# Chunked attention and a SoLU feed-forward: two single rows instead of four, two more units transposed on TensorE, one run per partition for q, k, v, few fillers, a new order of steps

## The chip, the cores and the metric

The kernel runs on one core of one Trainium2 chip. The metric is device time in microseconds of one execution. Before the change three runs gave 383.9, 387.94 and 388.43 us, median 387.94. Names of engines: PE is TensorE (PEld its weight loads), DVE VectorE, ACT ScalarE, POOL GpSimd; SP is the engine that issues nearly all DMAs.

## The reference

Attention over chunks, then a feed-forward layer, on 4 x 768 = 3072 tokens of width 512 (8 heads of 64):

```python
for c in range(nc):                       # 32 queries at a time
    k_ctx = k[:, :, l_start:r_end]        # 16 keys to the left, 8 to the right of the chunk
    k_full = np.concatenate([mem_k, k_ctx], axis=2)          # and 8 memory keys
    v_full = np.concatenate([mem_v, v_ctx], axis=2)
    scores = scale * np.matmul(q_c, k_full.transpose(0, 1, 3, 2))
    a = softmax(scores)
    out[:, :, c_start:c_end] = np.matmul(a, v_full)
...
h = x @ w_in                              # x: 3072 x 512, w_in: 512 x 1024
sm = softmax(h)
solu = h * sm
ln = (solu - mean) / np.sqrt(var + 1e-06) * g_ln
return ln @ w_out                         # w_out: 1024 x 512
```

The two weight matrices arrive as 64-bit floats, 4 MB each; everything else is 32-bit.

## The kernel before, in words

The 3072 tokens are 24 rows of tiles of 128 tokens. In the attention part an item is one row (items 0 to 3) or two rows (items 4 to 13). In the feed-forward part the unit is always one row, t = 0 to 23. The whole program is straight-line code: a string `ORDER` (line 29) lists about a thousand steps by short names, and the loop at line 569 issues them in just that order. So the order of instructions on each engine's queue is the order of the string, and each engine works through its own queue strictly in turn, waiting on semaphores where a step needs data or a free buffer.

Attention, for item i: `Lq`, `Lk`, `Lv` load q, k and v (SP, line 226). `S` computes the scores, 32 small fp32 matmuls per row (line 347; each shows as two matmul and two weight-load instructions). `M`, `Bm`, `X`, `Z` are the row maximum, its subtraction, the exponential (ScalarE) and the reciprocal row sum. The probabilities are then transposed: either on TensorE (`PT`, line 333, and a copy `PC` out of PSUM), or, for paired items, by VectorE in 32 x 32 blocks (`Pt`, line 304), a write to DRAM (`Pw`, line 312) and four reads of 128 KB that put the blocks in place (`Pr`, line 320). `V` multiplies by v (line 415), `N` normalises. The result x is transposed in the same two ways (`XT`, or `Xt`, `Xw`, `Xr`), and `XH`, `XL` round it to a high part and a residual.

Feed-forward, for row t: `Gt.c.half` are the hidden matmuls, a group of three per step (high x high, high x low, low x high; line 480), 8 groups per row. `Hm`, `He`, `Hu` are maximum, exponential and product; `C` centres; the row is transposed on TensorE (`UT`, rows 0 to 3) or through DRAM (`Ut`, `Uw`, `Ur`); `UH`, `UL` split it; `Ot.f` are the projection matmuls, 8 groups of three (line 540); `Sq`, `Dn` make the variance and its root, `Os` scales the result (line 548) and `St` stores it, from ScalarE's queue.

Weights: `D` loads a piece (SP), `A` packs its upper words (ScalarE, line 261), `B` shifts (line 268) and `I` inserts the lower words (VectorE, line 273), `H` and `L` split it into a rounded part and a residual (lines 214, 217, 282). The pieces are two halves of w_in's first chunk of 128 rows, its three other chunks, and four pairs of w_out's blocks.

`Wu n` are fillers: n multiplications of a zero tile by itself (line 201), each of which shows as two matmul instructions. A letter behind @ names the engine of a step that can run on several: V VectorE, S ScalarE, G POOL.

Of the kernel before, what the change touches and what calls it, by code (L numbers as in the profile page):

```python
# [11 lines left out]
F32 = mybir.dt.float32  # L12
# [6 lines left out]
P = 128  # L19
# [4 lines left out]
SINGLES = 4  # L24
# [5 lines left out]
CT Lk0 Wu18 Lq0 S0 M0 Bm0 Wu19 D0 A0 B0 I0 H0.0@G L0.0@G X0 Z0 PT0 PC0@S D1 A1 Lq2 Lk2 S2 M2 Bm2 X2  # L30
B1 I1 H1.0@G Z2 Lk1 Lq1 S1 M1 D4 A4 B4 I4 Wu36 Lv0 D2 A2 Lk3 V0 Wu28 Bm1 L1.0@G N0 B2 Lq3 I2 H2.1@G
XT0 XH0@S Lv2 S3 PT2 PC2@S H4.0@G M3 XL0@V V2 Bm3 G0.0.0 X1 PT1 Z1 G0.0.1 X3 PT3 H2.0@G N2 PC1@S
PC3@S Lv1 Z3 D3 V1 A3 N1 L2.0@G G0.1.0 B3 I3 L4.0@G Lv3 V3 N3 XT2 XH2@S XL2@V XT1 L2.1@G Lk4 Lq4
G0.1.1 S4 M4 XH1@S XL1@V H3.0@G G2.0.0 G2.0.1 G2.1.0 H3.1@S D6 A6 XT3 XH3@S Bm4 D7 H4.1@G L3.0@G
L3.1@G G0.2.0 G0.2.1 B6 XL3@V G1.0.0 I6 X4 Pt4 D5 A5 B5 I5 G2.1.1 G2.2.0 G2.2.1 Lg H5.1@S G1.0.1
L4.1@G L5.1@G G2.3.0 G2.3.1 Hm2 He2 D8 A8 Z4 G1.1.0 G1.1.1 G1.2.0 G1.2.1 Hu2 G0.3.0 C2@G G0.3.1 A7
H6.1@S G1.3.0 H5.0@S G1.3.1 Hm0 He0 H6.0@S Lv4 B7 Pw4 I7 G3.0.0 G3.0.1 G3.1.0 Lk5 G3.1.1 Pr4 H7.1@S
G3.2.0 G3.2.1 G3.3.0 L6.0@G Hm1 Hu0 He1 Lv6 L7.1@G Lk6 L5.0@G Hu1 C1@S G3.3.1 Hm3 He3 V4 N4 Lq5 UT1
UH1@S Hu3 Wu1 UL1@V C0@S Xt4 Lq6 Xw4 Xr4 S5 S6 O1.0 O1.1 H7.0@S C3@S UT3 M5 Bm5 UH3@S UL3@V X5 Pt5
# [50 lines left out]
def chunked_attention_then_solu_kernel(  # L90
# [23 lines left out]
    NT, _, NP_, _ = qT.shape  # L114
    items = [(t, 1) for t in range(SINGLES)] + [(t, 2) for t in range(SINGLES, NT, 2)]
    LINE = kw.shape[3]
    NCH, D = vw.shape[3], vw.shape[4]
    KEYS = vw.shape[1] // 2
    DM, DF = w_in.shape
# [66 lines left out]
    w_in32 = w_in.bitcast(U32).rearrange("(c p) (f two) -> c p f two", p=P, two=2)  # L186
    w_out32 = w_out.bitcast(U32).rearrange("(f p) (e two) -> f p e two", p=P, two=2)
# [41 lines left out]
    PIECES = [("in", [(0, 0)]), ("in", [(0, 1)])]  # L229
    PIECES += [("in", [(c, 0), (c, 1)]) for c in range(1, NC_)]  # L230
    PIECES += [("out", [f, f + 1]) for f in range(0, NF, 2)]
    rest = [sum(len(parts) == 2 for _, parts in PIECES)]

    def width(i):
        return HALF * len(PIECES[i][1])

    def part(i, k):
        matrix, parts = PIECES[i]
        if matrix == "out":
            f = parts[k]  # L240
            return w_out_h[:, f], w_out_l[:, f], f
        c, half = parts[k]
        s = slice(half * HALF, (half + 1) * HALF)
        return w_in_h[:, c, s], w_in_l[:, c, s], None

    def pairs(ap):
        return ap.bitcast(U32).rearrange("p (n two) -> p n two", two=2)

    def w_load(i):
        matrix, parts = PIECES[i]  # L250
        raw = take("raw" if len(parts) == 2 else "slot", ("raw", i), 2)
        if matrix == "out":
            raw = raw.bitcast(U32).rearrange("p (f n two) -> p f n two", f=2, two=2)
# [387 lines left out]
```

## Time and profile before

| | us |
|---|---|
| median of three runs | 387.94 |
| the profiled execution, its own time | 389.14 |
| its span, first to last instruction | 387.3 |
| TensorE busy in the span | 353.5 |
| VectorE, ScalarE, POOL busy | 221.4, 131.9, 132.3 |
| weight loads of TensorE busy | 289.9 |
| DMA: moved, mean rate | 84.43 MB, 218 GB/s |

The profile is one execution. Busy time counts an instruction from its start to its end; a fused stretch in the timeline shows the start, the length, the engine, the line, the tiles written and read and how many instructions it holds, and in square brackets how long the engine was idle before it and what released it. "issue" stands for idle time in which the engine waited for no semaphore. In the chain of waits each piece is what the end of the program waited for, followed back in time. The granted clock is TensorE's, 1.00 for full speed.

### The profile page before, as it was taken

Reading aid. Unit: us, or ns where it says so; the run is one execution under the profiler, and the core shown is the slowest. Engines: PE = TensorE matmul, PEld = TensorE weight load, DVE = VectorE, ACT = ScalarE, POOL = GpSimd, SP = SyncE. Lnnn points to the kernel's source line nnn. Section 1 sums busy time; section 2 is a strip of 40 time slices with the busy share of each in tenths; the row PEclk is TensorE's granted clock in tenths of the full one; section 3 lists DMA queues with packets and bytes.
Section 4 is the critical chain, followed back from the end, with each engine's and each line's share of the span. In section 5 each row is a group of like instructions: output and inputs, shape, how many; then the busy total and the mean of one; then the engine's idle time right before and its main releaser. Section 6 shows DMA issues by size and latency. Waiting matters only on the chain.

```text
span 387.3 us, 10357 instructions
## 1 busy us (share of the span) xinstructions
PE 353.5 (91%) x4502; PEld 289.9 (75%) x4502; DVE 221.4 (57%) x274; ACT 131.9 (34%) x190; POOL 132.3 (34%) x175
## 2 busy tenths in 40 slices
PE   8998999598949999799979958996898999999996
PEld 8997787486737887587858846884786888888875
DVE  0744899486865777477858483553555524546400
ACT  2314558253343221341535240322262024533311
POOL 0314537306032313440253342402233464455540
PEclk9999999899986999899979996999799999999999
DMA  7997676358496896489997774496535365257241
GB/s 229 418 410 302 218 217 257 112 172 279 159 336 209 261 304 186 149 276 334 291 306 241 227 228 146 190 274 189 153 110 204 124 204 156 89 207 254 82 164 55
DMA packets 44141, 84.43 MB, mean 218 GB/s; under 512 B 4544, under 2 KB 25024, under 8 KB 43712
## 3 DMA queue, kind: packets, MB, share of 16 engines
q1 hardware_dynamic: 40640, 77.48, 60.8%
q10 hardware_dynamic: 3456, 6.29, 4.5%
q8 instruction: 35, 0.57, 0.6%
q14 instruction: 10, 0.08, 0.1%
HBM read 56.50 MB, written 27.26 MB: 216 GB/s over the span
## 4 chain that ended last, share of the span: by engine, by line
PE 58%; DMA 19%; DVE 7%; issue 6%; POOL 4%; SPq 3%; ACT 2%; ACTq 0%; DVEq 0%; POOLq 0%
PE two L480 23%; PE one L540 19%; PE two L201 7%; PE two L347 5%; DMA v<-in_vw 4%; DMA out<-half 4%; PE two L415 4%; DMA raw<-u_away 3%; SPq L320 2%; DVE fr L217 2%; DVE raw L304 2%; DMA u_away<-raw 1%; DMA slot<-u_away 1%; DMA k<-in_kw 1%; POOL fr L217 1%
## 5 line engine op out<-in xcount | busy, mean ns | idle before, releaser
L540 PE MATMUL one<-w_out_h,fr 128*128 128x512 f32 x384 | 140.8, 407 | 9.8 <-issue 6.0
L480 PE MATMUL two<-w_in_h,fr 128*128 128x512 f32 x384 | 140.8, 405 | 4.3 <-POOL fr L214 2.9
L480 PEld LDWEIGHTS two<-w_in_h,fr 128*128 128x128 f32 x384 | 74.8, 195 | 27.0 <-issue 5.4
L540 PEld LDWEIGHTS one<-w_out_h,fr 128*128 128x128 f32 x384 | 74.4, 194 | 26.0 <-issue 4.2
L480 PE MATMUL two<-w_in_l,fr 128*128 128x512 f32 x192 | 77.1, 402 | 0.0
L540 PE MATMUL one<-w_out_l,fr 128*128 128x512 f32 x192 | 76.8, 400 | 0.0
L489 DVE TENSOR_REDUCE per_row<-two 128x1 f32<-128x1024 f32 x24 | 29.2, 1216 | 37.0 <-PE two L480 37.0
L540 PEld LDWEIGHTS one<-w_out_l,fr 128*128 128x128 f32 x192 | 37.4, 195 | 10.1 <-issue 2.7
L480 PEld LDWEIGHTS two<-w_in_l,fr 128*128 128x128 f32 x192 | 37.5, 195 | 7.6
L548 ACT ACTIVATE half<-one,per_row 128x512 f32<-128x512 f32 x24 | 16.5, 687 | 54.8 <-PE one L540 41.0
L494 ACT ACTIVATE raw<-two,per_row 128x1024 f32<-128x1024 f32 x16 | 17.8, 1114 | 46.3 <-DVE per_row L489 46.3
L347 PE MATMUL two<-k,q 64*32 64x64 f32 x1536 | 19.6, 232 | 12.3 <-issue 7.1
L201 PE MATMUL two<-z 128*128 128x128 f32 x214 | 28.3, 296 | 1.2 <-DVE z L190 1.0
L214 POOL TENSOR_SCALAR fr<-slot 128x1024 fp32r<-128x1024 f32 x11 | 12.7, 1158 | 46.9 <-DMA slot<-x_away 24.5
L201 PEld LDWEIGHTS two<-z 128*128 128x128 f32 x214 | 27.3, 210 | 1.8 <-DVE z L190 1.0
L504 DVE CUSTOM_DVE_ANT_0 raw<-two,raw 128x1024 f32<-128x1024 f32 x16 | 19.4, 1215 | 15.8 <-ACT raw L494 15.7
L214 POOL TENSOR_SCALAR fr<-raw 128x1024 fp32r<-128x1024 f32 x7 | 7.4, 1053 | 60.0 <-DMA raw<-x_away 20.1
L347 PEld LDWEIGHTS two<-k,q 64*32 64x32 f32 x1536 | 16.7, 108 | 12.2 <-issue 9.9
L370 DVE TENSOR_REDUCE per_head<-two 128x16 f32<-128x1024 f32 (+1 forms) x14 | 15.0, 1068 | 17.0 <-PE two L347 16.7
L217 POOL TENSOR_TENSOR fr<-raw,fr 128x1024 fp32r<-128x1024 f32 x7 | 16.8, 2399 | 22.3 <-ACT fr L212 13.8
L217 POOL TENSOR_TENSOR fr<-slot,fr 128x1024 fp32r<-128x1024 f32 x9 | 21.5, 2387 | 7.9 <-PE two L480 7.2
L212 ACT CAST fr<-raw 128x1024 fp32r<-128x1024 f32 x8 | 8.3, 1046 | 41.7 <-DMA raw<-x_away 13.8
(89 smaller groups left out, 395.8 us busy)
## 6 DMA issues: line engine op xcount, KB each, us to landing
v<-in_vw SPq DMA_DIRECT2D x10, 1024.0 KB, 7.8
k<-in_kw SPq DMA_DIRECT2D x10, 672.0 KB, 7.1
out<-half ACTq DMA_DIRECT2D x24, 256.0 KB, 2.9
q<-in_qT SPq DMA_DIRECT2D x10, 512.0 KB, 7.9
u_away<-raw SPq DMA_DIRECT2D x10, 512.0 KB, 4.2
raw<-u_away SPq DMA_DIRECT2D x40, 128.0 KB, 3.4
u_away<-slot SPq DMA_DIRECT2D x10, 512.0 KB, 3.5
slot<-u_away SPq DMA_DIRECT2D x40, 128.0 KB, 3.2
```

Of the source, the lines that this page charges most:

```text
L201: nc.tensor.matmul(z_ps, z, z, start=True, stop=True)
L214: nc.gpsimd.tensor_scalar(out, in_, 1.0, 0.0, ALU.mult, ALU.add)
L217: (nc.gpsimd if on == "G" else nc.vector).tensor_tensor(out, a, b, ALU.subtract)
L347: nc.tensor.matmul(s[32 * j:32 * j + 32, r, t, g], q[rows, o + t, g, 32 * j:32 * j + 32], k[rows, o + t, g, START[j]:START[j] + KEYS], sta ...
L370: nc.vector.tensor_reduce(nmax, s, axis=AX.X, op=ALU.max, negate=True)
L415: nc.tensor.matmul(x[32 * j:32 * j + 32, r, t, g], pT[rows, t, g, j], vv[rows, o + t, g, j], start=True, stop=True,)
L480: nc.tensor.matmul(h[:, half], x[a], w[b][:, c, half * HALF:(half + 1) * HALF], start=c == 0 and i == 0, stop=c == NC_ - 1 and i == 2,)
L489: nc.vector.tensor_reduce(take("per_row", ("hm", t), 1), flat(get("h", t)), axis=AX.X, op=ALU.max, negate=True)
L494: nc.scalar.activation(take("slot", ("u", t), 2), flat(get("h", t)), AF.Exp, bias=get("hm", t), scale=1.0, accum_out=take("per_row", ("esu ...
L504: nc.vector.tensor_tensor_reduce(u, flat(get("h", t)), u, 1.0, 0.0, ALU.mult, ALU.add, accum_out=usum)
L540: nc.tensor.matmul(get("o", t), u[a], w[b][:, f], start=f == 0 and i == 0, stop=f == NF - 1 and i == 2)
L548: nc.scalar.mul(take("half", ("osb", t), 1), get("o", t), get("rstd", t))
```

## The change

- `SINGLES` goes from 4 to 2: items 0 and 1 are single rows, items 2 to 12 pairs of rows. So item numbers above 1 mean other rows than before.
- Items 0 to 3 still go over TensorE for both transposes (`PT`, `XT`), but items 2 and 3 are pairs now: six rows instead of four. UT stays at rows 0 to 3.
- w_in's first chunk is loaded in one piece and packed, shifted and inserted in two halves (`SPLIT`).
- The host lays out q, k and v so that what one load brings to a partition is one run in DRAM; two neighbouring rows of w_out, 4 KB each, go to one partition, so a piece of w_out is one run per partition too, and w_in's columns and g are permuted to match.
- `ORDER` is written anew throughout. Fillers fall from 107 to 10 (214 to 20 matmul instructions).

```diff
-SINGLES = 4
+SINGLES = 2
+SPLIT = {0: 2}
 ORDER = """
-CT Lk0 Wu18 Lq0 S0 M0 Bm0 Wu19 D0 A0 B0 I0 H0.0@G L0.0@G X0 Z0 PT0 PC0@S D1 A1 Lq2 Lk2 S2 M2 Bm2 X2
...
+D0 CT A0.0 B0.0 A0.1 Lq0 B0.1 I0.0 H0.0@S Lk0 S0 M0 Lq2 Lk2 Bm0 Lk1 Lq1 X0 I0.1 H0.1@S L0.0@G Wu5 Z0
...
-    w_in32 = w_in.bitcast(U32).rearrange("(c p) (f two) -> c p f two", p=P, two=2)
-    w_out32 = w_out.bitcast(U32).rearrange("(f p) (e two) -> f p e two", p=P, two=2)
+    w_in32 = w_in.bitcast(U32).rearrange("(c p) f -> c p f", p=P)
+    w_out32 = w_out.bitcast(U32).rearrange("(k p s) e -> k p (s e)", p=P, s=2)
...
-    def load(name, src, dims):
+    def load(name, src):
         def step(i):
             t, n = items[i]
             buf = shared(name, (name, t // 2), 3 - n)
-            o = t % 2
-            nc.sync.dma_start(buf[:, o:o + n], src[t:t + n].rearrange(dims))
+            size = src.shape[0] // NT
+            line = size // P
+            flat_buf = buf.rearrange("p t a b -> p (t a b)") if len(buf.shape) == 4 else \
+                buf.rearrange("p t a b c -> p (t a b c)")
+            o = t % 2 * line
+            nc.sync.dma_start(
+                flat_buf[:, o:o + n * line],
+                src[t * size:(t + n) * size].rearrange("(p e) -> p e", p=P),
+            )
         return step
...
     def w_load(i):
-        matrix, parts = PIECES[i]
-        raw = take("raw" if len(parts) == 2 else "slot", ("raw", i), 2)
...
+        raw = take("raw", ("raw", i), 2 * SPLIT.get(i, 1)).bitcast(U32)
+        nc.sync.dma_start(raw, w_in32[i] if i < NC_ else w_out32[i - NC_])
 
-    def w_pack(i):
-        a = take("slot" if width(i) == W else "half", ("a", i), len(PIECES[i][1]))
+    def w_pack(i, x):
+        a = shared("slot", ("a", i), 2)
         nc.scalar.activation(
-            a, pairs(get("raw", i))[:, :, 1].bitcast(F32), AF.Prelu, scale=2.0**-112, alpha=-(2.0**32)
+            cut(a, i, x), cut(words(i, 1), i, x).bitcast(F32), AF.Prelu,
+            scale=2.0**-112, alpha=-(2.0**32),
         )
         used("raw", i)
...
+    def by_item(x):
+        n = x.shape[0]
+        late = x[SINGLES:].reshape((n - SINGLES) // 2, 2, P, -1).transpose(0, 2, 1, 3)
+        return np.concatenate([x[:SINGLES].ravel(), late.ravel()])
...
+    column = np.arange(DF).reshape(-1, P, 2).transpose(0, 2, 1).ravel()
+    g = moe_g_ln[column].reshape(-1, P).T
```

How the order moves the instructions shows at three places. First, TensorE at the start of the program (`z` is the zero tile of the fillers, `two` and `one` are PSUM tiles, x32 is one row's S or V, x64 a pair's). Before:

```order
L201 MATMUL two0_88<-z_171 128x128 x18
L347 MATMUL two0_88<-k0_95,q0_93 32x64 x32
L201 MATMUL two1_89<-z_171 128x128 x19
L333 MATMUL one0_91<-ident_168,half0_70 128x128 x4
L347 MATMUL two1_89<-k1_96,q1_94 32x64 x32
L347 MATMUL two2_90<-k0_95,q0_93 32x64 x32
L201 MATMUL two0_88<-z_171 128x128 x36
L415 MATMUL two0_88<-v0_97,half2_72 32x64 x32
L201 MATMUL two1_89<-z_171 128x128 x28
L333 MATMUL one1_92<-ident_168,half1_71 128x128 x4
```

Now:

```order
L347 MATMUL two0_88<-k0_95,q0_93 32x64 x32
L203 MATMUL two1_89<-z_171 128x128 x5
L347 MATMUL two1_89<-k1_96,q1_94 32x64 x64
L333 MATMUL one0_91<-ident_168,half0_70 128x128 x4
L347 MATMUL two2_90<-k0_95,q0_93 32x64 x32
L333 MATMUL one1_92<-ident_168,half1_71 128x128 x4
L415 MATMUL two0_88<-v0_97,half2_72 32x64 x32
L203 MATMUL two1_89<-z_171 128x128 x5
L333 MATMUL one0_91<-ident_168,half4_74 128x128 x4
L415 MATMUL two1_89<-v0_97,half3_73 32x64 x32
```

The fillers of 36 and 28 ahead of and behind the first V (line 415) are gone, and the transpose of the first x (the last row before, the last but one now) follows it after five fillers.

Second, ScalarE in the same stretch (line 261, now 260, packs a weight piece; line 212, now 214, copies or casts). Before:

```order
L261 ACTIVATE slot3_66<-raw1_77 128x1024
L212 CAST fr0_80<-one1_92 128x512
L212 COPY half0_70<-one0_91 128x512
L383 ACTIVATE half5_75<-half5_75 128x512
L383 ACTIVATE half2_72<-half2_72 128x512
L212 COPY half1_71<-one0_91 128x512
L212 COPY half4_74<-one1_92 128x512
L261 ACTIVATE slot4_67<-raw2_78 128x1024
```

Now:

```order
L260 ACTIVATE slot3_66<-raw2_78 128x1024
L214 COPY half3_73<-one1_92 128x512
L383 ACTIVATE slot2_65<-slot2_65 128x1024
L214 CAST fr0_80<-one0_91 128x512
L214 CAST w_in_h_163<-slot3_66 128x512
L260 ACTIVATE slot4_67<-raw3_79 128x1024
```

The pack of the last w_in chunk (the last row of each) stood behind the cast of the first x and five more steps, and now stands behind that cast and one more.

Third, TensorE where the fifth and sixth paired item's scores are computed. Before:

```order
L415 MATMUL two0_88<-v0_97,slot0_63 32x64 x64
L333 MATMUL two1_89<-ident_168,raw1_77 128x128 x8
L201 MATMUL two0_88<-z_171 128x128
L347 MATMUL two0_88<-k1_96,q1_94 32x64 x64
L347 MATMUL two2_90<-k0_95,q0_93 32x64 x64
```

Now, around one of them:

```order
L540 MATMUL one0_91<-w_out_h_165,fr6_86 128x512
L347 MATMUL two0_88<-k0_95,q0_93 32x64 x64
L480 MATMUL two2_90<-w_in_h_163,fr5_85 128x512
L480 MATMUL two2_90<-w_in_l_164,fr5_85 128x512
L480 MATMUL two2_90<-w_in_h_163,fr7_87 128x512
```

Two paired S stood side by side behind a paired V and eight transposes; now each S and V has groups of 512 columns on both sides.

## Rows read from the trace of the kernel before

**Rows 1.** The page: busy us, share of the span, instructions; an instruction queue's packets, MB, share.

```profile
PE 353.5 (91%) x4502; PEld 289.9 (75%) x4502; DVE 221.4 (57%) x274; ACT 131.9 (34%) x190; POOL 132.3 (34%) x175
...
q8 instruction: 35, 0.57, 0.6%
```

**Rows 2.** Span and mean granted clock of the core.

```profile
core 0: 387.3 us, clock 0.952
```

**Rows 3.** Timeline of TensorE, the start: start us, us, what, count.

```profile
1.04 7.18 PE L201 MATMUL two<-z 128*128 128x128 f32 x36 [1.04 <-DVE z L190]
...
8.93 4.51 PE L201 MATMUL two<-z 128*128 128x128 f32 x38
...
24.62 6.52 PE L201 MATMUL two<-z 128*128 128x128 f32 x56
```

**Rows 4.** The chain that ended last: start us, us, what.

```profile
46.40 17.05 PE two L480 x75
...
373.76 9.36 PE one L540 x40
```

**Rows 5.** Timeline of TensorE: transposes, a V, and rows with idle before them.

```profile
70.09 1.45 PE L347 MATMUL two<-k,q 64*32 64x64 f32 x125 [1.87 <-issue]
...
74.92 0.40 PE L540 MATMUL one<-w_out_h,fr 128*128 128x512 f32 x1 [2.48 <-issue]
...
104.65 1.03 PE L333 MATMUL two<-ident,slot 128*128 128x128 f32 x8
...
106.31 1.48 PE L415 MATMUL two<-v,slot 64*32 64x64 f32 x128
...
116.83 0.26 PE L347 MATMUL two<-k,q 64*32 64x64 f32 x1 [4.60 <-issue]
...
157.34 0.80 PE L540 MATMUL one<-w_out_h,fr 128*128 128x512 f32 x1 [2.15 <-issue]
...
198.58 0.79 PE L540 MATMUL one<-w_out_h,fr 128*128 128x512 f32 x1 [2.34 <-ACT fr L212]
...
232.46 2.05 PE L347 MATMUL two<-k,q 64*32 64x64 f32 x128 [3.94 <-DMA q<-in_qT]
...
235.92 0.80 PE L540 MATMUL one<-w_out_h,fr 128*128 128x512 f32 x1 [1.40 <-issue]
...
269.85 0.72 PE L480 MATMUL two<-w_in_h,fr 128*128 128x512 f32 x1 [2.94 <-POOL fr L214]
```

**Rows 6.** Timeline of ScalarE: the first x's cast, the last w_in chunk's pack.

```profile
31.61 0.59 ACT L212 CAST fr<-one 128x512 fp32r<-128x512 f32 x1 [10.04 <-PE one L333]
...
38.09 1.12 ACT L261 ACTIVATE slot<-raw 128x1024 f32<-128x1024 f32 x1
```

**Rows 7.** Stretches of 10 us: each engine's busy us (count), clock, DMA share, GB/s.

```profile
0.00:10.00 10.00, 8.96 (x109) 8.75 (x110) 1.02 (x3) 2.18 (x3) 0.72 (x7) 1.00 0.72 234
10.00:20.00 10.00, 9.88 (x202) 9.48 (x202) 7.81 (x16) 3.50 (x5) 3.78 (x4) 1.00 1.03 418
20.00:30.00 10.00, 10.00 (x147) 9.79 (x147) 4.17 (x5) 1.16 (x1) 2.48 (x4) 1.00 1.03 410
```

**Rows 8.** DMA issues: count, KB each, median us from issue to landing.

```profile
x_away<-raw SPq DMA_DIRECT2D x5, 512.0 KB, 4.4
raw<-x_away SPq DMA_DIRECT2D x20, 128.0 KB, 2.8
```

**Rows 9.** Instructions by line and shape: count, busy us, mean ns, idle before.

```profile
L261 ACT ACTIVATE slot<-raw 128x1024 f32<-128x1024 f32 x6 | 6.9, 1150 | 2.6 <-DMA raw<-in_w_in 2.6
L273 DVE SCALAR_TENSOR_TENSOR slot<-raw,slot 128x1024 uint32<-128x1024 uint32 x6 | 7.3, 1222 | 0.1
L304 DVE STREAM_TRANSPOSE raw<-slot 128x1024 f32<-128x1024 f32 x10 | 12.3, 1235 | 2.6 <-DMA v<-in_vw 1.3 <-ACT slot L514 1.2
L217 POOL TENSOR_TENSOR w_in_l<-slot,w_in_h 128x512 fp32r<-128x512 f32 x6 | 7.5, 1276 | 0.1
```

**Rows 10.** Timeline of VectorE: the last row's maximum, the first step behind its hidden layer.

```profile
354.25 1.23 DVE L489 TENSOR_REDUCE per_row<-two 128x1 f32<-128x1024 f32 x1 [3.12 <-PE two L480]
```

More of the change, by code (lines that the diff above doesn't have):

```diff
@@ L35 @@
[L35 to L39, printed above, removed]
@@ new lines @@
+G1.1.1 I6.0 XT2 XH2@S XL2@V He0 Lg H4.0@S H4.1@S L4.1@G G1.2.0 G1.2.1 G1.3.0 Hu0 G1.3.1 Hm1 He1 S3
+M3 Bm3 G3.0.0 G3.0.1 G3.1.0 G3.1.1 D5 D7 G3.2.0 G2.0.0 G3.2.1 Hu1 G3.3.0 G3.3.1 A5.0 B5.0 X3 PT3
+C0@S I5.0 G2.0.1 G2.1.0 C1@G A7.0 Lv3 PC3@S V3 G2.1.1 G2.2.0 G2.2.1 L4.0@G Hm3 He3 Z3 Lv5 Hu3 C3@S
+UT3 UH3@S N3 XT3 B7.0 XH3@S I7.0 G2.3.0 G2.3.1 UL3@V O3.0 Lk4 H5.0@S Lq4 S4 XL3@V G4.0.0 G4.0.1 O3.1
+G4.1.0 G4.1.1 H6.0@S Hm2 He2 Lq5 M4 Bm4 UT0 Lv4 Sq3 G4.2.0 Hu2 Lk6 X4 Pt4 H5.1@S Lk5 S5 G4.2.1 UH0@S
@@ L113, in chunked_attention_then_solu_kernel @@
     nc = tc.nc
-    NT, _, NP_, _ = qT.shape
+    D = P // 2
+    NP_ = w_in.shape[0] // (2 * D)
+    NT = out.shape[0] // P
+    NCH = P // CHUNK
+    LINE = kw.shape[0] // (NT * P * NP_)
+    KEYS = P // 2
+    DM, DF = w_in.shape
     items = [(t, 1) for t in range(SINGLES)] + [(t, 2) for t in range(SINGLES, NT, 2)]
[L116 to L119, printed above, removed]
     NC_ = DM // P
@@ L224, in step @@
             buf = shared(name, (name, t // 2), 3 - n)
-            o = t % 2
-            nc.sync.dma_start(buf[:, o:o + n], src[t:t + n].rearrange(dims))
-        return step
[L229 to L235, printed above, removed]
-    def part(i, k):
-        matrix, parts = PIECES[i]
[L239 to L244, printed above, removed]
@@ new lines, in load, with cut, words @@
+        return step
+    rest = [2 * NC_]
+    def part(i, k):
+        if i < NC_:
+            s = slice(k * HALF, (k + 1) * HALF)
+            return w_in_h[:, i, s], w_in_l[:, i, s], None
+        f = 2 * (i - NC_) + k
+        return w_out_h[:, f], w_out_l[:, f], f
+    def cut(ap, i, x):
+        n = ap.shape[1] // SPLIT.get(i, 1)
+        return ap[:, x * n:(x + 1) * n]
+    def words(i, k):
+        return get("raw", i).bitcast(U32).rearrange("p (n two) -> p n two", two=2)[:, :, k]
+    def w_load(i):
+        raw = take("raw", ("raw", i), 2 * SPLIT.get(i, 1)).bitcast(U32)
+        nc.sync.dma_start(raw, w_in32[i] if i < NC_ else w_out32[i - NC_])
@@ L623 @@
     qT, kw, vw = _layout(q, k, v, mem_k, mem_v)
-    g = moe_g_ln.reshape(-1, P).T
-    w_in, w_out = (np.ascontiguousarray(w).view(np.uint64) for w in (moe_w_in, moe_w_out))
+    DF = moe_g_ln.shape[0]
+    column = np.arange(DF).reshape(-1, P, 2).transpose(0, 2, 1).ravel()
+    g = moe_g_ln[column].reshape(-1, P).T
+    w_in, w_out = (np.ascontiguousarray(w).view(np.uint64) for w in (moe_w_in[:, column], moe_w_out))
     ins = dict(zip(_INS, (qT, kw, vw, w_in, w_out, g)))
```

123 lines of the change are left out of this document (56 added, 67 removed).

## The prediction

> **What bounds the kernel now.** [...] Then I read the chain of waits and the timeline, to cut the span in two:
>
> - *The start, to 46.4 us.* There the chain begins one unbroken run of 75 matmuls [rows 4]. Before it TensorE is "busy" mostly with 202 fillers, multiplications of a zero tile, the last 56 from 24.6 to 31.1 us [rows 3]. They hold up the useful steps behind them in TensorE's queue. ScalarE shows it: the cast of the first x waits 10.0 us for TensorE and starts at 31.6; the pack of the last w_in chunk stands behind it in ScalarE's order and starts only at 38.1 [rows 6], though by the sum of loads below the chunk itself was there at about 24.
> - *From 46.4 to the last matmul at 383.1* (373.76 + 9.36 [rows 4]) 336.7 us pass.
>
> The work left at 46.4, counted off the order: 377 groups of three hidden or projection matmuls, 9 paired S, 10 paired V, 32 transposes. A group takes 17.05 / 25 = 0.682 us [rows 4], a pair's S or V 1.48, a transpose 1.03 / 8 = 0.13 [rows 5]. That is 257.1 + 28.1 + 4.1 = 289.3 us. Idle: 33.8, less 1.0 before the first filler, 4.2 after the last matmul and some 1.4 in small waits before 46.4, leaves 27.2. [...] After the last matmul come 4.2 us of scaling and store.
>
> The idle falls in two kinds. *Issue*, where no semaphore is waited for: 1.87, 2.48, 4.60, 2.15, 1.40, together 12.5 us [rows 5]. All five stand inside or right behind S or V steps that follow one another closely. TensorE's queue holds 4502 matmuls and as many weight loads; the instruction queue moved 35 packets [rows 1], one per 257 instructions, and one paired S or V alone is 256 of them in 1.48 us. I read these waits as the next packet not being there. *Late data* is the other 14.7: 2.34, 3.94 and 2.94 are the longest [rows 5].
>
> **The change part by part.**
>
> *Fillers.* 214 become 20. Their busy time is worth nothing by itself, since it covered waiting. What counts is that nothing stands before the first V and the first x any more.
>
> *The start.* Loads pace it now. Up to the last w_in chunk the new SP order moves 7488 KB = 7.67 MB (the old one 8.19). The queue carried 2.34 MB to 10 us, 4.18 in the next ten, then 0.41 per us, with the engines full (share 1.03) [rows 7]. So that chunk lands at 20 + (7.67 - 6.52) / 0.41 = 22.8 us. (The same sum for the old order gives 24.1.) Behind it: pack 1.15, shift about 0.75 (an estimate, 0.6 of the insert), insert 1.22, round 0.63 (an estimate, half the pack), residual 1.28 [rows 9], 5.0 in all, and some 2 for queueing on VectorE and POOL: the dense run starts at 30. Bounds: 27 (no queueing) and 34 (the first x's cast, now behind the pack of the chunk before, late too). Work left there: 186 + 192 groups, ten paired S and V each, 56 transposes, 24 of which (PT3, XT2, XT3) stood before the dense run in the old order: 257.8 + 29.6 + 7.3 = 294.7 us.
>
> *Two more units on TensorE.* 16 transposes more (a row pair's p and x): 2.1 us, in the sum above. In exchange VectorE loses two block transposes, and SP two writes and eight reads with their round trips.
>
> *One run per partition.* The queue carried 0.41 to 0.42 MB per us with runs of 2 to 4 KB [rows 7], so I price runs of 4 to 8 KB at nothing; after 40 us TensorE hides these loads anyway. The permuted w_in columns and g are made on the host.
>
> *The new order, issue waits.* I cut TensorE's instructions into blocks of 256 and summed the work in each by the durations above. A wait is what the next packet takes less what the block lasts. In the timeline a packet took about 3.4 us (from the S before to 70.1) to 4.8 (from there to 74.9). In the old order eight blocks after 46.4 last under 3.5 us, the shortest 1.4, twice; the rule gives 6 us of waits at 3.4 and 20 at 4.8, and the measured 12.5 is the middle. In the new one no two S or V are adjacent, four late blocks last 2.6 to 3.4 us, and the rule gives 1 and 8. I take 4. [...]
>
> *The new order, late data.* A round trip through DRAM, from V to the first hidden matmul: two VectorE passes of 1.2 (as the transpose of [rows 9]), a write of 4.4, four reads that land 2.8 us after their issue [rows 8] and are issued one behind the other (2.8 to 4.6 in all, an estimate), cast and residual 2.4 to 3.6 (an estimate: two to three such passes): 12.0 to 15.0. The old order leaves 13.4 to 15.8 us of TensorE work there for five of ten items, the new one 14.4 for one and 16.3 or more for eight. From the hidden layer to the projection the last row took 354.25 to 373.76 = 19.5 us [rows 10, 4]; the new order's tightest have 18.4 (the last row) and 19.2. Short by 1 to 3 us each: item 4's V and its first hidden step, the k load of item 5, which must wait for item 4's scores and has 5.1 us of work to hide under, and the last row. I take 8 for 14.7; bounds 3 and 18, since loads also queue behind each other on SP in ways that an order does not show.
>
> *Clock.* [...] At the start the first 36 fillers took 199 ns each and the next 38 took 119 [rows 3], so the array started slow and ran at full speed after some 8 us of work. Without fillers the first groups pay that: 2.5 us. [...]
>
> **Sum.** 30 + 294.7 + 4.7 change-overs + 12 idle + 9.5 clock + 4.2 end = 355.1 against the span of 387.3. The profiled run's own time is 389.1, 1.8 over its span and 1.2 over the median of the runs shown, so **355.7**.
>
> **Rivals.**
> - *The start is gained, the waits come back* in new places at the old size: 30 + 294.7 + 4.7 + 27.2 + 18 + 4.2 = 378.8, so 379.4. For it: the new order is packed much as tightly as the old. Against: less traffic, longer slacks, spaced S and V. 0.15.
> - *Not code.* The issue waits have another cause and stay: 8.5 more idle, 5 more clock: 369. Against: the arithmetic of blocks above. 0.10.
> - *The start is not gained*, because the chain of ScalarE and VectorE steps sets it, not loads and fillers: dense at 42, so 368. For it: the last chunk's pack is still behind the first x's cast on ScalarE. 0.08.
> - *Slower: code starves.* Instruction packets share the DMA engines with the loads, and the new order has no fillers to wait in. One packet took 9.0 us (from the end of the V at 107.8 to 116.83 [rows 5]). [...] Against: at 7 us the rule would give the old order 48 us of issue waits, and 12.5 were measured. 0.07.
>
> That leaves 0.60 for the forecast, whose own range is 342 to 368. A measurement of this kernel tells about 2% (7.8 us) from no change; the three runs shown spread over 4.5. Faster means under 380.2: the forecast, the second and third rivals, and half of the first, so 0.85; same 0.08; slower 0.07. The range goes from 27 + 294.7 + 4.7 + 4 idle + 5 clock + 4.2, 340 as a run, to the first rival's 379.5; about 2 in 10 are left out.
>
> **What would show it.** In the new profile: a first hidden matmul near 23 us and an unbroken TensorE from 30; issue waits under 8 us in all and none over 3; a mean clock of 0.95 or better in spite of the slow start; idle after 30 near 12 us. [...]

## The result and the profile after

The changed kernel took 356.69 us (median of four runs, 355.58 to 359.48) against 388.19 for the kernel before: a ratio of 0.922 [0.913, 0.931], the 95% interval in brackets. 355.7 had been forecast. The profiled execution is the slowest of the four: 359.48 us, span 357.7. Medians take in every execution; ratios leave out those that the record marks as slow (one of four in runs 2 and 5 below, two of four in run 3, three of five in run 6, three of four in run 10), and the profiles of runs 6 and 10 are of such executions.

The page of the changed kernel (busy us, share of the span, instructions; an instruction queue's packets, MB, share):

```profile
PE 325.8 (91%) x4324; PEld 263.7 (74%) x4324; DVE 219.7 (61%) x264; ACT 130.0 (36%) x189; POOL 138.9 (39%) x173
...
q8 instruction: 34, 0.56, 0.6%
```

Against [rows 1] TensorE's busy time fell by 27.7 us, 23.4 of it fillers (28.3 before, 4.9 now); VectorE and ScalarE are busy some 2 us less than before, POOL 6.6 more. Span and mean granted clock, for [rows 2]:

```profile
core 0: 357.7 us, clock 0.970
```

TensorE's timeline: every wait over 0.5 us behind the first matmul, stretches of the start, and the first hidden groups (start us, us, what; in brackets the idle before and its releaser):

```profile
17.32 0.73 PE L347 MATMUL two<-k,q 64*32 64x64 f32 x49 [3.63 <-issue]
21.22 1.11 PE L333 MATMUL one<-ident,half 128*128 128x128 f32 x4 [3.18 <-ACT half L383]
22.27 1.18 PE L415 MATMUL two<-v,half 64*32 64x64 f32 x64
23.38 2.37 PE L203 MATMUL two<-z 128*128 128x128 f32 x10
...
26.11 0.86 PE L415 MATMUL two<-v,half 64*32 64x64 f32 x64
...
28.19 0.48 PE L480 MATMUL two<-w_in_h,fr 128*128 128x512 f32 x1
28.50 0.39 PE L480 MATMUL two<-w_in_l,fr 128*128 128x512 f32 x1
...
34.51 0.61 PE L480 MATMUL two<-w_in_h,fr 128*128 128x512 f32 x2
35.31 0.50 PE L480 MATMUL two<-w_in_l,fr 128*128 128x512 f32 x1 [0.19 <-DVE w_in_l L219]
...
111.86 0.27 PE L415 MATMUL two<-v,raw 64*32 64x64 f32 x2 [1.42 <-DMA raw<-p_away]
112.97 1.52 PE L415 MATMUL two<-v,raw 64*32 64x64 f32 x126 [0.84 <-DMA raw<-p_away]
...
142.99 0.50 PE L480 MATMUL two<-w_in_h,fr 128*128 128x512 f32 x1 [0.65 <-DVE per_row L504]
...
161.83 1.92 PE L347 MATMUL two<-k,q 64*32 64x64 f32 x128 [3.29 <-DMA q<-in_qT]
...
192.15 1.46 PE L415 MATMUL two<-v,slot 64*32 64x64 f32 x126 [0.71 <-DMA slot<-p_away]
...
199.80 0.50 PE L480 MATMUL two<-w_in_h,fr 128*128 128x512 f32 x1 [1.44 <-POOL fr L219]
...
262.91 1.22 PE L480 MATMUL two<-w_in_h,fr 128*128 128x512 f32 x2 [4.12 <-DVE fr L219]
```

Read it against [rows 5]: behind the start not one wait for issue is left, where five long ones stood. The late data are still there, in other places: 12.9 us with two short ones (0.19 and 0.24). The first hidden matmul came at 28.2 us and the start is dense from 34.5, both later than forecast. Two engines show why. VectorE, then ScalarE:

```profile
13.25 1.17 DVE L370 TENSOR_REDUCE per_head<-two 128x16 f32<-128x1024 f32 x1
18.08 0.69 DVE L370 TENSOR_REDUCE per_head<-two 128x8 f32<-128x512 f32 x1 [3.66 <-PE two L347]
```

```profile
20.54 0.63 ACT L383 ACTIVATE half<-half 128x512 f32<-128x512 f32 x1 [5.01 <-DVE half L377]
21.07 0.57 ACT L214 COPY half<-one 128x512 f32<-128x512 f32 x1
...
26.22 0.59 ACT L214 CAST fr<-one 128x512 fp32r<-128x512 f32 x1 [0.73 <-PE one L333]
...
27.22 1.19 ACT L260 ACTIVATE slot<-raw 128x1024 f32<-128x1024 f32 x1
```

S1 waited 3.63 us in its middle for issue. VectorE's next step was the maximum of S1, so it stood still for 3.66 us with the subtraction of S2 ready behind it; ScalarE stood 5.01, with a copy ready. Even so the first x's cast waited 0.73 us for TensorE where it had waited 10.0, and the last w_in pack came at 27.2 where it had come at 38.1 [rows 6]. The clock, in stretches of 10 us (each engine's busy us and count, clock, DMA share, GB/s):

```profile
10.00:20.00 10.00, 4.41 (x202) 3.61 (x201) 6.17 (x9) 2.34 (x3) 1.34 (x2) 0.93 1.03 423
20.00:30.00 10.00, 8.78 (x166) 7.72 (x167) 8.87 (x12) 7.77 (x11) 5.48 (x6) 0.73 1.01 414
...
110.00:120.00 10.00, 7.74 (x148) 5.93 (x148) 6.74 (x9) 3.98 (x9) 6.11 (x14) 0.83 0.60 197
160.00:170.00 10.00, 8.17 (x268) 6.83 (x271) 6.07 (x8) 3.16 (x5) 2.73 (x3) 0.83 1.04 358
260.00:270.00 10.00, 7.09 (x21) 5.64 (x22) 6.21 (x7) 1.78 (x3) 1.77 (x1) 0.66 0.45 162
```

In the traces before and after, every record of the clock is 0.5 or 1.00. The three late stretches hold 3.4, 3.4 and 6.8 us at 0.5, from 114.22, 162.01 and 261.00 us on, each in or just behind one of the longer waits (they end at 112.97, 161.83 and 262.91). In the last a group of three took 1.28 us (263.93 to 265.21) and behind it 0.69 (269.20 to 269.89). About 2 us of it are idle, so the low clock costs some half of 11.6: 5.8 us (an estimate from these records and lengths).

The first two rows hold another 6.8 us at 0.5, from 18.65 to 25.48 us, behind the waits of 3.63 and 3.18 us with 0.73 us of work between them. In that stretch V0 took 1.18 us, where V1 at 26.11 took 0.86; a row's transposes took 1.11, where the next at 25.58 took 0.60; and ten filler matmuls took 237 ns each, for 119 in the second stretch of [rows 3]. Together that is some 2.0 us (an estimate from these rows). TensorE did not stand still from 21.2 to 32.6, so the start came later by about as much.

### The profile page after: what moved, and what is told of

It is laid out like the page before. It is cut to its first block, busy times and chain, and to the rows that moved or that the text cites. A ratio compares the mean times of both kernels' runs of the same rounds, so it can differ in the third digit from the quotient of the medians.

```text
span 357.7 us, 9973 instructions
## 1 busy us (share of the span) xinstructions
PE 325.8 (91%) x4324; PEld 263.7 (74%) x4324; DVE 219.7 (61%) x264; ACT 130.0 (36%) x189; POOL 138.9 (39%) x173
## 4 chain that ended last, share of the span: by engine, by line
PE 61%; DMA 18%; DVE 12%; SPq 3%; ACT 3%; issue 2%; POOL 1%; DVEq 0%; POOLq 0%; ACTq 0%
PE one L540 28%; PE two L480 23%; DMA out<-half 5%; PE two L347 4%; PE two L415 3%; SPq L320 3%; DMA q<-in_qT 2%; DMA raw<-p_away 2%; DMA k<-in_kw 2%; DVE per_head L387 2%; DMA p_away<-raw 2%; DMA raw<-x_away 1%; DMA slot<-x_away 1%; PE two L203 1%; PE two L333 1%
## 5 line engine op out<-in xcount | busy, mean ns | idle before, releaser
L480 PE MATMUL two<-w_in_h,fr 128*128 128x512 f32 x384 | 143.0, 405 | 6.8 <-DVE fr L219 4.6
L540 PE MATMUL one<-w_out_h,fr 128*128 128x512 f32 x384 | 138.1, 396 | 0.1
L489 DVE TENSOR_REDUCE per_row<-two 128x1 f32<-128x1024 f32 x24 | 29.1, 1212 | 28.9 <-PE two L480 28.8
L219 POOL TENSOR_TENSOR fr<-raw,fr 128x1024 fp32r<-128x1024 f32 x13 | 31.2, 2403 | 17.4 <-ACT fr L214 16.6
L216 POOL TENSOR_SCALAR fr<-raw 128x1024 fp32r<-128x1024 f32 x11 | 11.6, 1051 | 47.1 <-DVE slot L304 18.1
L494 ACT ACTIVATE slot<-two,per_row 128x1024 f32<-128x1024 f32 x12 | 13.4, 1118 | 30.6 <-DVE per_row L489 30.6
L494 ACT ACTIVATE raw<-two,per_row 128x1024 f32<-128x1024 f32 x12 | 13.4, 1115 | 27.7 <-DVE per_row L489 21.4
L216 POOL TENSOR_SCALAR fr<-slot 128x1024 fp32r<-128x1024 f32 x8 | 8.4, 1052 | 32.4 <-DMA slot<-u_away 15.3
L504 DVE CUSTOM_DVE_ANT_0 slot<-two,slot 128x1024 f32<-128x1024 f32 x12 | 14.7, 1222 | 8.1 <-ACT slot L494 8.1
L504 DVE CUSTOM_DVE_ANT_0 raw<-two,raw 128x1024 f32<-128x1024 f32 x12 | 14.5, 1206 | 7.7 <-ACT raw L494 6.2
L304 DVE STREAM_TRANSPOSE raw<-slot 128x1024 f32<-128x1024 f32 x10 | 12.4, 1238 | 8.1 <-POOL slot L516 5.9
## 6 DMA issues: line engine op xcount, KB each, us to landing
raw<-in_w_in SPq DMA_DIRECT2D x4, 1024.0 KB, 11.3
```

What stands on the lines that cost most here:

```text
L216: nc.gpsimd.tensor_scalar(out, in_, 1.0, 0.0, ALU.mult, ALU.add)
L219: (nc.gpsimd if on == "G" else nc.vector).tensor_tensor(out, a, b, ALU.subtract)
L304: nc.vector.transpose(t, src.rearrange("p (m d n) -> p d m n", d=4, n=SQ))
L480: nc.tensor.matmul(h[:, half], x[a], w[b][:, c, half * HALF:(half + 1) * HALF], start=c == 0 and i == 0, stop=c == NC_ - 1 and i == 2,)
L489: nc.vector.tensor_reduce(take("per_row", ("hm", t), 1), flat(get("h", t)), axis=AX.X, op=ALU.max, negate=True)
L494: nc.scalar.activation(take("slot", ("u", t), 2), flat(get("h", t)), AF.Exp, bias=get("hm", t), scale=1.0, accum_out=take("per_row", ("esu ...
```

## The experiments

The kernel before had medians of 388.19 to 391.8 us on different chips, 0.9% apart, so ratios to the kernel before on the same chip are compared, or kernels that shared a chip.

**1. The kernel before without its fillers at the start.**

```diff
-CT Lk0 Wu18 Lq0 S0 M0 Bm0 Wu19 D0 A0 ...  I4 Wu36 Lv0 ... V0 Wu28 Bm1
+CT Lk0 Lq0 S0 M0 Bm0 D0 A0 ...  I4 Lv0 ... V0 Bm1
```

> The kernel before, with the four blocks of fillers of the start (18, 19, 36 and 28) taken out and nothing else changed. If the fillers held up the start, as the prediction says: the last w_in chunk lands at about 24 us, the steps behind it take 7 and the old order is denser in TensorE steps that wait for each other, so the unbroken run starts at 33 to 40 us instead of 46.4, and the time is 375 to 381 us; the clock gives back up to 2.5 of it. If loads or the chain of ScalarE and VectorE steps set the start anyway: 386 to 390 us. The issue waits of the middle stay in both, since S5 and S6 are still side by side.

378.92 us against 391.8: ratio 0.968 [0.963, 0.973]. The chain of this kernel has the run of 75 matmuls of [rows 4] again, 6.7 us earlier (39.69 for 46.40):

```profile
39.69 17.05 PE two L480 x75
```

The mean clock rose too, to 0.964 in its profiled run from 0.953, the mean of the runs before on that chip. By these means the share of the clock that was not granted is (1 - 0.953) x 392 = 18.4 us before and (1 - 0.964) x 377 = 13.6 now, so at most some 5 of the 12.9 us are clock behind the start (an estimate); the start itself is in neither mean (see the last section). Work that does nothing is not free cover: it stood before useful steps. The issue waits stayed (11.3 us in all, 2.2 of them ahead of the run of 75), as expected; late data rose from 14.7 to 19.2.

**2. The kernel before with S and V spaced.** S6, S8, S11 and V11 moved by two to four groups:

```diff
-... S5 S6 O1.0 O1.1 ... O1.2 O1.3 UT0 ...
+... S5 O1.0 O1.1 ... O1.2 O1.3 S6 UT0 ...
```

> The kernel before, with four TensorE steps moved by a few groups so that no two S or V are close: S6 two groups on (away from S5), S8 three (away from V6), S11 behind V8 and two more groups (away from S10), V11 three (away from S13). If the issue waits are the code of TensorE that comes too late, the wait inside S6 goes and the others shrink: 12.5 us of issue waits become 3 to 9, the clock follows by 1 to 4, and the time is 377 to 384 us. If they have another cause: 386 to 390 us, with the five issue waits as before.

388.16 us against 391.8: 0.988 [0.980, 0.996], 3.6 us less by the medians, where 4 to 11 had been expected. TensorE's timeline:

```profile
66.52 1.45 PE L347 MATMUL two<-k,q 64*32 64x64 f32 x124 [0.38 <-issue]
69.98 0.50 PE L540 MATMUL one<-w_out_l,fr 128*128 128x512 f32 x1 [0.88 <-issue]
...
140.63 0.50 PE L540 MATMUL one<-w_out_h,fr 128*128 128x512 f32 x1 [2.57 <-POOL fr L214]
...
157.49 0.33 PE L347 MATMUL two<-k,q 64*32 64x64 f32 x11 [1.72 <-issue]
...
269.51 0.79 PE L480 MATMUL two<-w_in_h,fr 128*128 128x512 f32 x1 [5.34 <-POOL fr L214]
```

The issue waits fell from 12.5 to 6.8 us as the theory said (1.87 and 2.48 in and behind S5 and S6, the second and third pair of the old kernel, became 0.38 and 0.88 in and behind S5), but late data rose from 14.7 to about 24. I read that as TensorE reaching the next round trips earlier and waiting for them; the run does not separate it from what the moved steps delay. In the old order spacing alone buys little: the waits came back, which is the prediction's first rival.

**3 and 4. Doubled scores, doubled hidden groups.** In the changed kernel the same TensorE time is added once in many small matmuls, once in few wide ones:

```diff
-        for t in range(n):
+        for t in list(range(n)) * (2 if i in (6, 7, 8, 9, 10, 11) else 1):
```

```diff
+        if c == 0 and t in (8, 10, 12, 14, 16, 18):
+            for i, (a, b) in enumerate(((0, 0), (0, 1), (1, 0))):
+                nc.tensor.matmul(
+                    h[:, half], x[a], w[b][:, c, half * HALF:(half + 1) * HALF], start=i == 0, stop=i == 2,
+                )
```

> The changed kernel, with the score matmuls of items 6 to 11 issued twice (256 more TensorE instructions each, the same results). The work itself is 6 x 1.48 = 8.9 us. If code comes at 3.4 to 4.8 us per 256 instructions, each doubled S holds a block that lasts 1.5 us and so waits 1.9 to 3.3 us more: 11 to 20 us of issue waits, 2 to 6 of clock, 378 to 391 us. If the issue waits of the kernel before were not code: 8.9 us for the work and no issue wait, 363 to 367 us.

> The changed kernel, with the first two hidden groups of rows 8, 10, 12, 14, 16 and 18 issued twice: 12 groups of 0.682 us, 8.2 us of TensorE work as in the run with doubled scores, but only 72 more instructions. Both theories: 362 to 366 us and no issue wait after the start; it is what the doubled scores are held against. If it costs as much as the doubled scores, added work of any kind does, and not the number of instructions.

384.77 us for the scores (ratio 0.974 [0.964, 0.983]) and 360.46 for the groups (0.922 [0.917, 0.927]), for 8.9 and 8.2 us of work. The scores' timeline has an issue wait at each doubled S (two in S6), seven in all, four of them here, and its page 40 packets, six more for 6 x 256 instructions:

```profile
83.79 1.48 PE L347 MATMUL two<-k,q 64*32 64x64 f32 x128 [1.67 <-issue]
88.34 0.87 PE L347 MATMUL two<-k,q 64*32 64x64 f32 x36 [3.07 <-issue]
...
146.51 1.35 PE L347 MATMUL two<-k,q 64*32 64x64 f32 x75 [4.18 <-issue]
...
231.19 1.04 PE L347 MATMUL two<-k,q 64*32 64x64 f32 x80 [3.16 <-issue]
```

```profile
q8 instruction: 40, 0.66, 0.7%
```

The groups' has three, where none had been expected:

```profile
83.61 0.62 PE L347 MATMUL two<-k,q 64*32 64x64 f32 x36 [1.10 <-issue]
95.07 0.83 PE L415 MATMUL two<-v,slot 64*32 64x64 f32 x62 [2.70 <-issue]
...
168.40 1.09 PE L415 MATMUL two<-v,slot 64*32 64x64 f32 x86 [0.41 <-issue]
```

21.1 against 4.2 us of issue waits: what costs here is the number of instructions, 2.8 us for each S doubled. So the rival "not code" is refuted.

The kept traces show it directly, and beyond these two runs. They hold each packet of the instruction queue (16,384 bytes) with its time. In all fourteen profiles there are 67 waits for issue of 0.15 us or more on TensorE. Each stands where the number of instructions that TensorE's queue has issued (matmuls, weight loads and the few others) is 193 above a multiple of 256. In the trace before, the wait that ends at 70.09 us stands behind 2497 of them and the one that ends at 74.92 behind 2753; in the result's, the wait of 3.63 us stands behind 449. The ten waits in these two traces end 1.3 to 1.5 us after a packet has landed: the one of 3.63 us ends at 17.32, and the only packet before 20 us moved from 14.78 to 15.80.

The surprise is the other kernel: 8.2 us of added work cost next to nothing (0.922 is the unaltered ratio), where 362 to 366 us had been expected. It fell into waits: the late q is 1.87 instead of 3.29, the late residual 1.59 instead of 4.12, and the clock stayed up in the profiled run (0.976 to 0.989 in its four, 0.970 to 0.981 in the four of the result):

```profile
core 0: 357.8 us, clock 0.989
```

So what the new order still loses is late data, and the clock that falls with it.

**5. The layout of q, k and v undone.**

```diff
-                flat_buf[:, o:o + n * line],
-                src[t * size:(t + n) * size].rearrange("(p e) -> p e", p=P),
+                flat_buf[:, o:o + n],
+                src[t * size:(t + n) * size].rearrange("(t p e) -> p t e", t=n, p=P),
```

> The changed kernel with the layout of q, k and v undone: a pair's load brings two runs per partition again (of 2 to 4 KB) instead of one; everything else as changed. The prediction prices the layout at nothing: 355 to 359 us, a ratio of 0.915 to 0.93, v, k and q landing in about the time they take now (8.5, 6.8 and 7.8 us). If the longer runs are worth something, the loads of the start land later and the dense run starts 1 to 3 us later: 358 to 361 us.

Ratio 0.926 [0.921, 0.930]; the unaltered kernel had 0.922 [0.913, 0.931], and 0.923 [0.915, 0.932] on another chip (run 7). No difference can be measured; v, k and q land in 8.7, 7.2 and 7.6 us, for 8.5, 6.8 and 7.8. Nothing, as priced. The layout of w_out was not undone.

**6. Late data, first try; 7 and 8. The unaltered kernel and a second try on one chip.**

```diff
-... S12 M12 Bm12 X12 O12.6 Pt12 G19.3.0 O13.0 G19.3.1 XL11@V ...
+... S12 M12 Bm12 XL11@V X12 O12.6 Pt12 G19.3.0 O13.0 G19.3.1 ...
-... Lv8 X8 ...   Ut8 Lk10 Lq10 G11.3.0 ...   XL8@G ...   Pr6 V6 N6 Lk9 ... O2.2 Xt6
+... Lv8 Lk10 Lq10 X8 ...   Ut8 G11.3.0 ...   XL8@V ...   Pr6 Lk9 ... O2.2 V6 N6 Xt6
```

> The changed kernel with five steps moved, each at one of its late-data waits after the start: the last residual but one (XL11) ahead of the transpose that waits for ScalarE, on VectorE; XL8 on VectorE instead of POOL; the loads of k and q for item 10 right behind item 8's scores; V6 with N6 two groups later. If those waits are what the order still costs, 11.1 us of late data (4.12, 3.29, 2.26, 1.44) fall to about 2, and of the 5.8 us that the low clock still takes 2 to 5 go with them: 343 to 349 us by the scale of 388.2 for the kernel before, a ratio of 0.885 to 0.90. If waits only turn up elsewhere once these are gone (the first rival of the prediction): 353 to 358 us, 0.91 to 0.922.

354.04 us, ratio 0.896 [0.892, 0.901] from two executions, within what was expected. All four waits that it aimed at were gone or at 0.5 us; behind them V9 waited 2.06 us for its probabilities, just after 20 us with the DMA engines full (share 0.99), and V11 2.71. The second try moves item 10's v behind those reads, and V11 two groups on.

```diff
-... Lv10 Pr9 ...   G16.3.0 V11 O10.5 Hm17 G16.3.1 He17 Hu17 XH10@S
+... Pr9 Lv10 ...   G16.3.0 O10.5 Hm17 G16.3.1 He17 Hu17 V11 XH10@S
```

> The changed kernel itself, unaltered, beside the next three on one chip: a ratio of 0.915 to 0.925. Both theories say the same; it is the scale for the three others. Its profile shows whether the issue waits that the last two runs had in S6 and V5 (1.2 to 1.9 and 2.6 to 3.0 us) are there too, which the first profile of this kernel did not have.

> The changed kernel with the five moves of the run on late data, and two more at the waits that run showed behind them: the reads of item 9's probabilities ahead of the load of item 10's v, which in that run kept the DMA engines full (share 0.99) just before V9 waited 2.06 us for them; V11 two groups later. If late data is what the order costs, 9 to 13 us under the unaltered kernel, a ratio of 0.885 to 0.90. If the waits turn up elsewhere: 0 to 5 us under it.

360.04 us (359.02 to 361.10) and 351.65 (349.57 to 353.63): 8.4 us less, ratio of the medians 0.977, without overlap, where 9 to 13 had been expected. One long wait is left, at V10:

```profile
186.92 0.27 PE L415 MATMUL two<-v,slot 64*32 64x64 f32 x2 [3.62 <-DMA slot<-p_away]
```

The unaltered kernel's issue waits in S6 and V5 were 0.20 and 0.65 us here, 1.64 and 2.96 in run 5, whose order is the same, none in the first profile: how long one and the same wait lasts varies between runs.

**9. Spaced further.**

```diff
-... Hm4 Lq6 S6 Pw5 O0.4 He4 Lk7 Xw4 O3.4 G5.2.1 ... Bm6 S7 Hu4 O0.6 O3.5 ... Pr5 V5 O3.6 ... G5.3.1 Z5 N5 X6 O3.7
+... Hm4 Lq6 Pw5 O0.4 He4 Lk7 Xw4 O3.4 S6 G5.2.1 ... Bm6 Hu4 O0.6 O3.5 S7 ... Pr5 O3.6 ... G5.3.1 Z5 X6 O3.7 V5 N5
```

> The run before (late data) with S6, S7 and V5 two, two and five groups later, so that their blocks of 256 instructions last 4.7 us each instead of 3.4, 4.7 and 3.4; nothing else. If a packet takes 5 to 6 us there, as waits of 1.2 and 2.7 us on top of blocks of 3.4 say, these 3.9 us of issue wait fall to about 1, and the time by 2 to 5 us. If the issue waits there are not code, they stay: no change, within 1 us.

352.47 us, no change. It decides nothing: of the 3.9 us that it was to remove only 0.56 were there on this chip.

**10 and 11. The start.** First alone, then on top of 9:

```diff
-... D2 Lv2 S1 M1 Bm2 Bm1 X1 PT1 PC0@S B3.0 I3.0 V0 H3.0@G L3.0@G H3.1@S Wu5 D4 Z1 D6 A1.0 PC1@S X2 N0 XT0 V1
+... D2 Lv2 Bm2 PC0@S S1 B3.0 I3.0 H3.0@G L3.0@G H3.1@S A1.0 M1 Bm1 X1 V0 PT1 D4 D6 N0 XT0 Z1 B1.0 PC1@S XH0@S I1.0 X2 XL0@V ... V1
```

> The changed kernel with the start alone put in another order: on VectorE the subtraction for item 2 and the shift and insert of one w_in chunk stand ahead of the first step that waits for S1; on ScalarE the copy of the first transposed probabilities ahead of the second exponential and the pack of chunk 1 too; on TensorE V0 right behind S1, and five fillers fewer. S1 itself waits 3.63 us for code as before. If the start is late because VectorE and ScalarE stood idle behind that wait in their own order, V0 starts at 18 to 19 us instead of 22.3, the first hidden matmul at 22 to 24 instead of 28.2, the unbroken run at 29 to 31 instead of 34.5, and the time falls by 3.5 to 5.5 us: 351 to 353 us, a ratio of 0.905 to 0.91. If the packets of code set the pace there, V0, V1 or the first groups wait for the next packet, which the wait in S1 shows to take 4 us and more with the DMA engines full: an issue wait of 1 to 4 us between 18 and 26 us, and 354 to 357 us.

> The run before (late data, spaced) with the new start as well, where the second exponential now stands ahead of the pack of chunk 1 and the five fillers are back, in front of S1. If the start is set by the order of VectorE and ScalarE behind the code wait in S1: the first hidden matmul at 23 to 25 us instead of 28, and 3 to 6 us less than the run before. If the start's gain is lost again to waits behind it: within 2 us.

Alone: V0 at 17.8 us, the first hidden matmul at 24.38, no idle of TensorE over 0.2 us from 21.1 to 42.7, and no issue wait from 18 to 26, as the first theory says; but its runs spread from 355.77 to 366.52, so the time decides nothing. On top of 9: 351.32 us for 352.47, ranges that overlap, where 3 to 6 us had been expected. The early gain is real in the trace and hardly in the time: the first hidden matmul came at 25.89 us for 27.51 in run 9, but of these 1.6 us only 0.4 are left at the 16 transposes behind (56.07 for 56.46; 54.86 in run 12, which has the same start). This kernel's timeline has another wait for issue, 1.80 us up to 23.95, and its clock from 20 to 30 us is lower than the result's 0.73:

```profile
17.64 0.91 PE L347 MATMUL two<-k,q 64*32 64x64 f32 x55 [3.07 <-issue]
...
23.95 0.90 PE L333 MATMUL one<-ident,half 128*128 128x128 f32 x3 [1.80 <-issue]
```

```profile
20.00:30.00 10.00, 7.38 (x91) 5.88 (x92) 6.82 (x11) 5.81 (x8) 4.87 (x4) 0.59 1.01 414
```

Once the engines' order is mended, waits for issue and the low clock (0.59) hold up the start in this run, while the DMA engines are full (share 1.01). What each of them costs was not separated.

**12. V10 later.** V10, N10, Xt10 and Xw10 six groups on, in the kernel of 11:

```diff
-... Ur10 V10 N10 O9.1 Xr9 Xt10 Xw10 O6.6 ... G13.3.1 Hm13 He13
+... Ur10 O9.1 Xr9 O6.6 ... G13.3.1 Hm13 V10 N10 Xt10 Xw10 He13
```

> The run before (late data, spaced, new start) with V10, N10 and the transpose and write of item 10's x six groups (4.1 us) later, for the one long wait that was left: V10 waited 3.62 and 0.75 us for the reads of its probabilities, whose write had stood 5.8 us behind a store, and the clock was at 0.76 and 0.89 in the two stretches of 10 us behind it. What V10 feeds is read more than 40 us later. If that is so, 4 us of waits and 1 to 2 of low clock go: 345 to 348 us, a ratio of 0.883 to 0.892. If another wait takes its place: 350 to 352 us, 0.895 to 0.905.

353.19 us, 0.907 [0.902, 0.911]: no gain, where 345 to 348 had been expected. Another wait took its place, 5.5 us in these three rows:

```profile
191.56 0.50 PE L480 MATMUL two<-w_in_h,fr 128*128 128x512 f32 x1 [2.17 <-POOL fr L216]
192.82 0.50 PE L480 MATMUL two<-w_in_h,fr 128*128 128x512 f32 x1 [0.53 <-DVE fr L219]
197.25 0.80 PE L480 MATMUL two<-w_in_h,fr 128*128 128x512 f32 x1 [2.77 <-DVE slot L429]
```

I had moved the one that waits, and not the cause. SP's waits from 165 to 195 us (us in total, times, longest) name it:

```profile
SPq L312 <- DMA out<-half: 8.1, 1, 8.1
```

The write of item 10's probabilities stood 8.1 us behind a store that has nothing to do with it: the semaphore that this write waited for is the one that the store's landing updates. The traces of the kernel before and of the result have 276 and 262 DMAs, from SP and ScalarE, on eight semaphores each; 268 and 254 of them follow another on their semaphore, and none starts before that one has landed. All that SP had behind that write, item 8's reads among them, came late. Moving the store was not tried.

The fastest kernels run are 8 and 11, at 351.65 and 351.32 us, which can't be told apart: 2.3 and 2.4% under the changed kernel on the same chip.

## Why the prediction was right, and where not

The total was met by terms that err in both directions, and that they cancel to about 1 us is luck (us; "after" from the profiled run, but work left and change-overs are the forecast's, not measured there; clock and change-overs are estimates in all three):

| term | before | forecast | after |
|---|---|---|---|
| dense start | 46.4 | 30 | 34.5 |
| work left | 289.3 | 294.7 | 294.7 |
| change-overs | 4.7 | 4.7 | 4.7 |
| issue waits after it | 12.5 | 4 | 0 |
| late data | 14.7 | 8 | 12.9 |
| clock | 15.5 | 9.5 | 5.8 |
| end | 4.2 | 4.2 | 3.8 |
| sum | 387.3 | 355.1 | 356.4, span 357.7 |

- *Fillers.* Right: they held up the start, and run 1 takes 12.9 us out of the old kernel by that alone. It paid although without them TensorE was still slow at 23.5 us, where a V took 1.18 us for 0.86 (last section).
- *The start.* Mis-sized by 4.5 us, past its bound of 34. I let loads pace it and gave 2 us for queueing. The blocks of code were counted behind 30 us only; the early ones (128 + 256 + 128 instructions of S0, S2 and S1) wait too, 3.63 us, and VectorE and ScalarE stood still behind that wait in their order. The low clock that followed took some 2.0 us more.
- *Issue waits.* That they go with the number of instructions is shown by runs 3 and 4 (21.1 against 4.2 us). The size is the least sure number here: 0 in the profile of the result, 1.4 and 4.6 us in S6, V5 and S8 in runs 7 and 5. The forecast's 4 lies among them. The fourth rival's 9.0 us for one packet are a misreading: by the count of instructions in the trace that block was entered at 109.26 us (256 instructions ahead of the wait's end at 116.83), not at the end of the V, so it took 7.6.
- *Late data.* Mis-sized, 12.9 for 8: I had only the shortest slacks of the order, not VectorE's steps ahead of a residual (4.12) or SP's ahead of a load (3.29). Waits of 3 us or more for single data turned up at least as often as before, so this step failed: q is late by 3.29 where it was 3.94 in [rows 5], and the residual's 4.12 comes on top. Run 8 shows that these waits could be moved, and that they and the clock behind them were worth 8.4 us.
- *Clock.* Better than forecast in the table, less so in fact. The first hidden groups did not pay for a slow start: they follow each other in 0.69 us (28.50 and the next), with the clock at 1.00 from 25.48 on. V0, transposes and fillers before them paid some 2.0 of the 2.5 us, inside the 34.5 of the start. Behind the start 12.9 us of idle (12 forecast) came with 5.8 of clock: 0.45 us for each. The 15.5 before are an estimate: 37 us at 0.5 by the mean of [rows 2], some 6 of them idle, half of the rest; for 27.2 of idle that is 0.57, the scale of the clock terms in the prediction's sums.
- *Terms of the sum.* No run shows the 9.5 us of clock or the 4.7 of change-overs. For the clock the runs showed 5.8 behind the start and some 2.0 inside it, both estimates from lengths and clock records; change-overs were not measured in any run.
- *One run per partition.* Nothing, as priced; not told apart by run 5. Transposing two more units on TensorE was not tried by itself.

How much of the gain is the new order's and not the fillers': 0.922 against 0.968, or 4.8% of the time of a kernel without fillers. It is not spacing alone, which run 2 saw turned into late data. How the rest divides between the new places of loads and round trips and the two units on TensorE was not tried.

## What to carry to other kernels

Count instructions beside time: here 1536 more instructions in small matmuls (run 3) brought 21.1 us of issue waits, and 72 more in wide ones (run 4), for as much work, 4.2. A wait on one engine can cost again on each engine whose next step needs it (here 3.63 us on TensorE, 3.66 on VectorE, 5.01 on ScalarE); put there first what does not. When a wait moves and the time doesn't, look for what held the producer (8.1 us behind a store in run 12), and move that. Check a printed clock against the length of equal instructions (1.00 printed for a V of 1.18 us and one of 0.86 in run 1).

## What was not expected

- The clock that the profile prints for the start of run 1 is not the one that TensorE had. A stretch of 10 us, and lines of its timeline:

```profile
20.00:30.00 10.00, 9.26 (x215) 7.10 (x214) 7.16 (x13) 3.85 (x7) 5.52 (x6) 1.00 1.03 409
```

```profile
23.49 1.18 PE L415 MATMUL two<-v,half 64*32 64x64 f32 x64 [0.74 <-ACT half L212]
24.60 0.79 PE L480 MATMUL two<-w_in_h,fr 128*128 128x512 f32 x1
...
28.79 0.86 PE L415 MATMUL two<-v,half 64*32 64x64 f32 x64
29.58 0.50 PE L480 MATMUL two<-w_in_h,fr 128*128 128x512 f32 x1
```

  A V of 64 matmuls took 1.18 us and then 0.86, a hidden matmul behind a V 0.79 and then 0.50. So TensorE was slower at 24.6 us than at 28.8, although the row says 1.00. In the trace the first record of the clock stands at 28.34 us (at 7.13 before the change, at 11.82 in the result), and ahead of it the rows print 1.00. The kernel before, with its fillers, ran its first V in 0.86 us, the later length:

```profile
23.84 0.86 PE L415 MATMUL two<-v,half 64*32 64x64 f32 x64
```

  With the fillers TensorE was at that length at 23.84 us, without them at 23.49 it was not (1.18 us), and taking them out paid all the same.
- 8.2 us of work added in front of waits cost nothing that could be measured (0.922 and 0.923 for the kernel without it).
- The wait for issue in one and the same S and V ranged from 0 to 3 us from run to run.
- A write waited 8.1 us for an unrelated store, through a shared semaphore.
